# Summing squares along rows, with few idle products, at the head of an attention-and-GELU kernel

## The chip, the cores and the metric

One core of a Trainium2 chip (trn2). The metric is the device time of one execution in microseconds (us). Each version is run several times on the same chip as the version it is compared with; one execution is profiled, and every execution lists the mean clock granted to TensorE.

## The reference

Four batches of q, k, v with 6080 rows and 256 columns; then a two-layer network with a tanh GELU on all 24320 rows of the attention's output.

```python
qn = q / (np.linalg.norm(q, axis=1, keepdims=True) + 1e-06)   # norm of each column over 6080 rows
kn = k / (np.linalg.norm(k, axis=1, keepdims=True) + 1e-06)
s = kn.transpose(0, 2, 1) @ qn / tau                          # 256 x 256 scores
a = softmax(s)                                                # over the last axis
x = (v @ a).reshape(B * S, D)
h = x @ w_in                                                  # 256 -> 2048
out = gelu_tanh(h) @ w_out                                    # 2048 -> 256
```

Scores and weights can be merged (a @ w_in is 256 x 2048), so the long part of the kernel is two products per block of 512 rows. But the first block can start only when batch 0's scores are known, and these need every row of q and k of batch 0: their product G and the column sums of squares. That head is what the change is about.

## The kernel before

Batch 0 is loaded in ten chunks of 2, 12, 12, 5 (and a rest), 4, 4, 4, 2, 1, 1 slots of 128 rows. For each chunk VectorE casts q and k to bf16, ScalarE squares them, and TensorE adds k^T q to G (two products of 256 columns per slot) and the squares to `cols`. A column of sums is made by a product whose weights are the squares and whose moving operand is one column of ones:

```python
def col_sums(cols, x, ones, first, last):
    for m in range(4):                       # q and k, two halves of 128 columns each
        nc.tensor.matmul(cols[:, m : m + 1],
                         lhsT=x[m // 2][:, m % 2 * 128 : m % 2 * 128 + 128], rhs=ones, ...)

fillers = [0, 0, 0, 5, 6, 5, 4, 2, 1, 0]     # idle products, chunk by chunk

def keep_clock(n):                           # bf16, 512 columns, result unused
    ...
for n, ch in enumerate(first_chunks):
    ...                                      # casts on VectorE (GpSimd for k of chunks 6 and 7)
    ...                                      # squares on ScalarE (VectorE for q of 6 and 7)
    keep_clock(fillers[n])
    for s, rows in slots_of(ch, 128):
        gram(G, qkb, s, rows, ...)           # two products of 256 columns
    ...                                      # pairs of squares added on VectorE, then col_sums
```

The twelve-slot chunks have one tile for q and one for k. Then come the norms, the scaled scores, their transposes, exp, the first pieces of `aw` (softmax @ w_in), and the first block's products `hp`. v of block 0 is turned on TensorE into one PSUM tile of two halves of 512 columns, and the first pieces of aw are scaled in halves, VectorE and ScalarE by turns:

```python
vps = pH.tile([128, 2, 512], FP32, tag="h", name="vps")
...
nc.vector.tensor_copy(vT0[:, 0, :], vps[:, 0, :])
...
nc.scalar.activation(vT0[:, 1, :], vps[:, 1, :], AF.Copy)
...
for n, t, act in ((0, 0, False), (1, 0, True), (0, 1, True), (1, 1, False), (2, None, False), (3, None, False)):
    ...                                      # aw piece = ps * 1/row sum, on ACT where act, else on DVE
```

Later batches are prepared while the products of the batch before run, and are the same in both versions.

## Time and profile before

| | before |
|---|---|
| time, median of 3 runs | 753.54 us (753.44 to 753.94) |
| span of the profiled run | 751.6 us |
| TensorE busy | 727.2 us (97%) |
| the loads of q and k of batch 0 end | about 34.7 us |
| sums of squares end | 37.48 us |
| first four hp products issued (start of the products after them) | 42.50 us |

TensorE is "PE" in the profile, VectorE "DVE", ScalarE "ACT", GpSimd "POOL". In a line of the chain of waits the columns are start, length and the work. In a line of a window they are its bounds, its length, the busy time of PE, PEld, DVE, ACT and POOL (with the instructions started), and at the end PEclk (granted clock, 1.00 is full), the DMA share and GB/s. The last row of the table is the *mark* used below: from it on TensorE hardly rests (in the run before it is busy for 692.84 of the 697.50 us from the mark to 740 us), and 751.6 - 42.50 = 709.1 us follow it.

### The profile page before, as it was taken

How to read it: one execution, taken by the hardware profiler on the slowest of the kernel's cores; microseconds unless marked ns; L12 is line 12 of the kernel's file. 1: busy time of each engine (PE TensorE's matmuls, PEld its weight loads, DVE VectorE, ACT ScalarE, POOL GpSimd, SP SyncE). 2: the span in 40 equal slices, each digit the busy share in tenths (PEclk: the TensorE clock that was granted, in tenths of full speed). 3: DMA queues.
4: the chain of work that ended last, by engine and by line, in shares of the span. 5: the costliest groups of instructions: out<-in, count | busy, mean ns of one | idle time of the engine just before them, and what ended most of it. 6: DMA issues, size and time to landing. Idle time of an engine off the chain costs nothing.

```text
span 751.6 us, 12382 instructions
## 1 busy us (share of the span) xinstructions
PE 727.2 (97%) x5181; PEld 502.5 (67%) x5271; DVE 289.9 (39%) x513; ACT 419.6 (56%) x414; POOL 82.3 (11%) x159
## 2 busy tenths in 40 slices
PE   3899999999999999999999999999999999999998
PEld 2656667666666666766666666776666666666666
DVE  4643646463431645554341265555343011011011
ACT  5675555555556555555645555555564655555552
POOL 1161110101012102101001102010101000000000
PEclk9999999999999999999999999999999999999999
DMA  8979676613227685833325776671422533321111
GB/s 373 386 226 175 120 144 144 132 43 79 83 62 144 113 162 108 142 79 81 87 57 116 145 115 125 148 143 46 76 81 56 103 88 67 69 78 50 41 57 57
DMA packets 83111, 86.48 MB, mean 115 GB/s; under 512 B 58992, under 2 KB 61680, under 8 KB 82544
## 3 DMA queue, kind: packets, MB, share of 16 engines
q0 software_dynamic: 14480, 30.87, 25.9%
q1 hardware_dynamic: 68272, 54.49, 24.8%
q8 instruction: 41, 0.67, 0.4%
q10 hardware_dynamic: 304, 0.33, 0.1%
q14 instruction: 14, 0.11, 0.1%
HBM read 78.91 MB, written 24.90 MB: 138 GB/s over the span
## 4 chain that ended last, share of the span: by engine, by line
PE 96%; DMA 2%; issue 1%; DVE 1%; SPq 0%; ACT 0%; DVEq 0%
PE yp L572 44%; PE hp L646 43%; PE G L177 5%; DMA st<-in_k_dram 2%; PE ps L229 2%; PE idle L173 1%; PE cols L189 0%; PE yp L677 0%; DVE qk L277 0%; SPq L83 0%; PE T L399 0%; DVE vT L404 0%; DVE Gs L207 0%; ACT aw L440 0%; PE vps L391 0%
## 5 line engine op out<-in xcount | busy, mean ns | idle before, releaser
L650 ACT ACTIVATE g<-hp 128x1024 bf16<-128x1024 f32 (+1 forms) x384 | 389.4, 1014 | 305.9 <-PE hp L646 292.0
L572 PE MATMUL yp<-wout_bf,g 128*128 128x256 bf16 x3024 | 392.0, 273 | 1.0
L646 PE MATMUL hp<-vT,aw 128*128 128x512 bf16 (+1 forms) x1453 | 383.3, 377 | 3.8 <-ACT aw L440 0.2
L572 PEld LDWEIGHTS <-g 128*128 128x128 bf16 x3024 | 295.9, 98 | 113.4
L646 PEld LDWEIGHTS <-aw 128*128 128x128 bf16 x1536 | 150.0, 98 | 104.2 <-ACT aw L440 0.4
L589 DVE COPY ysb<-yp 128x512 f32<-128x512 f32 (+1 forms) x95 | 64.9, 683 | 393.9 <-PE yp L572 393.9
L489 DVE TENSOR_TENSOR acc<-acc,sq 128x512 f32<-128x512 f32 x141 | 97.6, 692 | 4.8
L488 DVE TENSOR_TENSOR sq<-qkb 128x512 bf16<-128x512 bf16 x141 | 58.9, 418 | 0.0
L177 PE MATMUL G<-qkb 128*128 128x256 bf16 x288 | 55.0, 273 | 0.0
L313 POOL DMA_DIRECT2D vb<-in_v_dram x47 | 25.9, 553 | 90.3 <-DMA vT<-vb 84.3
L338 POOL CAST gate<-g 1x1 f32<-1x1 bf16 x24 | 5.9, 244 | 232.8 <-ACT g L650 232.8
L235 DVE TENSOR_SCALAR aw<-ps,rsinv 128x512 bf16<-128x512 f32 x30 | 22.4, 749 | 22.2 <-PE ps L229 15.8
L177 PEld LDWEIGHTS <-qkb 128*128 128x128 bf16 x288 | 28.2, 98 | 3.3
L177 PE MATMUL G<-qk 128*128 128x256 bf16 x96 | 15.6, 324 | 14.7 <-DVE qk L277 14.7
L177 PEld LDWEIGHTS <-qk 128*128 128x128 bf16 x96 | 10.7, 115 | 18.8 <-DVE qk L277 14.9
L229 PE MATMUL ps<-win_bf,eT 128*128 128x512 bf16 x54 | 16.4, 379 | 0.1
L508 POOL TENSOR_TENSOR r<-r,half 128x4 f32<-128x4 f32 x3 | 3.1, 1040 | 101.6 <-DVE r L507 101.6
L279 ACT ACTIVATE sq<-st 128x3072 bf16<-128x3072 f32 (+2 forms) x6 | 10.6, 1768 | 5.8 <-DMA st<-in_k_dram 2.6
L83 POOL DMA_DIRECT2D qkb<-in_q_dram x24 | 12.8, 535 | 5.8 <-issue 4.3
L83 POOL DMA_DIRECT2D qkb<-in_k_dram x24 | 13.0, 542 | 0.0
L629 POOL COPY g<-gr 128x1024 bf16<-128x1024 bf16 x2 | 2.1, 1034 | 98.2 <-PE yp L572 98.2
L664 POOL COPY gr<-g 128x1024 bf16<-128x1024 bf16 x2 | 2.1, 1035 | 79.9 <-ACT g L650 79.9
(84 smaller groups left out, 137.8 us busy)
## 6 DMA issues: line engine op xcount, KB each, us to landing
out_dram<-ysb SPq DMA_DIRECT2D x44, 512.0 KB, 3.0
vb<-in_v_dram POOLq DMA_DIRECT2D x43, 256.0 KB, 6.6
qkb<-in_q_dram POOLq DMA_DIRECT2D x21, 384.0 KB, 4.6
qkb<-in_k_dram POOLq DMA_DIRECT2D x21, 384.0 KB, 6.4
vT<-vb SPq DMA_TRANSPOSE x184, 2.9
wst<-in_moe_w_out_dram SPq DMA_DIRECT2D x4, 512.0 KB, 10.4
g<-in_q_dram SPq DMA_DIRECT2D x1, 1536.0 KB, 6.8
g<-in_k_dram SPq DMA_DIRECT2D x1, 1536.0 KB, 10.0
```

The costliest lines, as they stand in the source:

```text
L83: engines[x].dma_start(out=dst[x][:, 0:size, :], in_=src[b, s0 * 128 : (s0 + size) * 128, :].rearrange("(p s) c -> p s c", s=size))
L177: nc.tensor.matmul(G[:, ic, :], lhsT=qk[1][:rows, s, ic * 128 : ic * 128 + 128], rhs=qk[0][:rows, s, :], start=first and ic == 0, stop=las ...
L229: nc.tensor.matmul(ps, lhsT=eT[:, jc, ic * 128 : ic * 128 + 128], rhs=win_bf[:, jc, fs * 512 : fs * 512 + 512], start=jc == 0, stop=jc == 1)
L235: nc.vector.tensor_scalar_mul(dst, sorted_columns(ps, fs), rsinv[:, ic : ic + 1])
L279: nc.scalar.activation(sq[:, 0:hi] if whole is None else sq, x, AF.Square)
L313: nc.gpsimd.dma_start(out=t[:, 0:n, :], in_=v_rows[r0 : r0 + n * 128, :].rearrange("(p s) c -> p s c", s=n))
L488: nc.vector.tensor_mul(sq[:rows], flat, flat)
L489: nc.vector.tensor_add(acc[:rows], acc[:rows], sq[:rows])
L572: nc.tensor.matmul(yp[:rows, at, :], lhsT=g[:, fc, s * 128 : s * 128 + rows], rhs=wout_bf[:, fc, :], start=fc == 0, stop=fc == FC - 1)
L589: nc.vector.tensor_copy(ysb[:, s0 : s + 1, :], yp[:, 0 : s + 1 - s0, :])
L646: nc.tensor.matmul(hp[:, j, :cols], lhsT=aw[:, cc, fc * 128 : fc * 128 + 128], rhs=vT[:, cc, :cols], start=cc == 0, stop=cc == 1)
L650: nc.scalar.activation(g[:, 2 * i : 2 * i + 2, :cols], hp[:, :, :cols], AF.Gelu_apprx_tanh)
```

## The change

The intent: the head's TensorE spends 23 idle products on its clock and many tiny products on sums. The change (1) sums the squares of chunks 0 to 4 along rows, one product of 512 columns per pair of slots with a column of ones as weights, copies the row out of PSUM once and turns it into columns by four fp32 products; (2) keeps three idle products, now fp32; (3) gives the twelve-slot chunks two tiles that hold q and k of six slots each; (4) does chunk 6's and 7's casts of k on VectorE, leaves chunk 7's square of q to ScalarE, and lets VectorE add the squares of chunks 4 and 5 in pairs too; (5) gives the halves of v block 0 own PSUM tiles and scales the first aw pieces whole. The change was also described with "later scores turned by DMA", but both versions do that alike. The core of the diff, with cuts:

```diff
-    fillers = [0, 0, 0, 5, 6, 5, 4, 2, 1, 0]
-    SQUARES_DVE = (6, 7)
-    CASTS_POOL = (6, 7)
+    IN_ROWS, SQUARES_DVE = 5, 6
+    fillers = [0, 0, 0, 1, 1, 1, 0, 0, 0, 0]
...
-    filler = const.tile([128, 512], BF16)
+    filler = const.tile([128, 1, 256], FP32)
...
+    row = pY.tile([128, 512], FP32, tag="y", name="row")[0:1, :].rearrange("p (x c) -> p x c", c=256)
+    row_sb = accp.tile([128, 2, 256], FP32, tag="acc", name="row_sb")[0:1]
...
+    def row_sums_of(parts):
+        nonlocal rowed
+        for x in parts:
+            nc.tensor.matmul(row, lhsT=ones_bf, rhs=x, start=rowed == 0, stop=rowed == n_sums - 1)
+            rowed += 1
+        if rowed == n_sums:
+            nc.vector.tensor_copy(row_sb, row)
+
+    def turn_rows():
+        for m in range(4):
+            nc.tensor.matmul(cols[:, m : m + 1], lhsT=row_sb[:, m // 2, m % 2 * 128 : m % 2 * 128 + 128],
+                             rhs=ones_f[0:1, :], start=m == 0, stop=False, skip_group_check=True)
...
+        qks = [qkp.tile([128, 2, SMAX, 256], BF16, tag="qk", name="qk") for _ in range(n_tiles)]
+        sqs = [sqp.tile([128, 2, SMAX, 256], BF16, tag="sq", name="sq") for _ in range(n_tiles)]
...
-    vps = pH.tile([128, 2, 512], FP32, tag="h", name="vps")
+    vps = [pH.tile([128, 2, 512], FP32, tag="h", name="vps")[:, 0, :] for _ in range(2)]
...
-    for n, t, act in ((0, 0, False), (1, 0, True), (0, 1, True), (1, 1, False), (2, None, False), (3, None, False)):
+    for n in range(4):
```

More of the change, by code (lines that the diff above doesn't have):

```diff
@@ L99 @@
     n_chunks = len(first_chunks)
-    TAIL = 4
-    fillers = [0, 0, 0, 5, 6, 5, 4, 2, 1, 0]
-    SQUARES_DVE = (6, 7)
-    CASTS_POOL = (6, 7)
-    def halves(pool, tag, dtype, size, most=SMAX):
-        tiles = [pool.tile([128, 2, most, 256], dtype, tag=tag, name=tag)
-                 for _ in range(1 if size <= most else 2)]
-        if len(tiles) == 1:
-            return [tiles[0][:, x] for x in range(2)], tiles[0]
-        return [t.rearrange("p a b c -> p (a b) c") for t in tiles], None
+    IN_ROWS, SQUARES_DVE = 5, 6
+    fillers = [0, 0, 0, 1, 1, 1, 0, 0, 0, 0]
     def slot_pair(whole, lo, hi):
@@ L167, in pieces @@
         return dst.rearrange("a (e t p) -> a e t p", p=128, t=t_of(fs))
-    def keep_clock(n, pool=pH, tag="h"):
+    def keep_clock(n):
         for _ in range(n):
-            idle = pool.tile([128, 2, 512] if pool is pH else [128, 512], FP32, tag=tag, name="idle")
-            nc.tensor.matmul(idle[:, 0, :] if pool is pH else idle, lhsT=filler[:, 0:128], rhs=filler, start=True, stop=True)
+            idle = pH.tile([128, 2, 512], FP32, tag="h", name="idle")
+            nc.tensor.matmul(idle[:, 0, :], lhsT=filler[:, 0, 0:128],
+                             rhs=filler.broadcast_to([128, 2, 256]), start=True, stop=True)
     def gram(G, qk, s, rows, first, last):
@@ L178, in gram @@
                 G[:, ic, :],
-                lhsT=qk[1][:rows, s, ic * 128 : ic * 128 + 128],
-                rhs=qk[0][:rows, s, :],
+                lhsT=qk[:rows, 1, s, ic * 128 : ic * 128 + 128],
+                rhs=qk[:rows, 0, s, :],
                 start=first and ic == 0,
@@ L239, with col_sums_of, pairs_of @@
     cols = pA.tile([128, 512], FP32, tag="a", name="cols")
-    seen, summed = 0, 0
-    def sums_of(parts, last):
-        nonlocal summed
+    row = pY.tile([128, 512], FP32, tag="y", name="row")[0:1, :].rearrange("p (x c) -> p x c", c=256)
+    row_sb = accp.tile([128, 2, 256], FP32, tag="acc", name="row_sb")[0:1]
+    n_sums = sum(-(-size // 2) + rem for _, size, rem in first_chunks[:IN_ROWS])
+    rowed = 0
+    def row_sums_of(parts):
[9 more added lines that the diff above has]
+                             rhs=ones_f[0:1, :], start=m == 0, stop=False, skip_group_check=True)
+    def col_sums_of(parts, last=False):
         for m, x in enumerate(parts):
-            col_sums(cols, x, ones_bf[: x[0].shape[0], :], summed == 0, last and m == len(parts) - 1)
-            summed += 1
-    def pairs_of(n, sqb):
-        size = first_chunks[n][1]
+            col_sums(cols, [x[:, y] for y in range(2)], ones_bf, False, last and m == len(parts) - 1)
+    def pairs_of(sq, size, rem):
         h = size // 2
-        pair, whole = halves(prp, "pair", BF16, h, SMAX // 2)
-        for x in range(2):
-            nc.vector.tensor_add(pair[x][:, 0:h], sqb[x][:, 0:h], sqb[x][:, h : 2 * h])
-        parts = [[y[:, s, :] for y in pair] for s in range(h)]
-        if size % 2:
-            parts.append([y[:, size - 1, :] for y in sqb])
-        if first_chunks[n][2]:
-            parts.append([y[:, size, :] for y in sqb])
-        sums_of(parts, False)
+        pair = prp.tile([128, 2, SMAX // 2, 256], BF16, tag="pair", name="pair")[:, :, 0:h]
+        nc.vector.tensor_add(pair, sq[:, :, 0:h], sq[:, :, h : 2 * h])
+        return [pair[:, :, s] for s in range(h)] + [sq[:, :, s] for s in range(2 * h, size + rem)]
+    seen = 0
     waiting = None
@@ L264 @@
         st, whole = staged[n]
-        size = ch[1]
-        qkb, qk_whole = halves(qkp, "qk", BF16, size)
-        sqb, sq_whole = halves(sqp, "sq", BF16, size)
-        hi = size + ch[2]
+        _, size, rem = ch
+        n_tiles = -(-size // SMAX)
+        each = size // n_tiles
+        hi = each + rem
+        qks = [qkp.tile([128, 2, SMAX, 256], BF16, tag="qk", name="qk") for _ in range(n_tiles)]
+        sqs = [sqp.tile([128, 2, SMAX, 256], BF16, tag="sq", name="sq") for _ in range(n_tiles)]
@@ L269 @@
         if whole is None:
-            todo = list(zip(qkb, sqb, st))
+            todo = [(x, t, st[x][:, t * each : t * each + each]) for x in range(2) for t in range(n_tiles)]
         else:
-            todo = [[y[:, :, 0:hi] for y in (qk_whole, sq_whole, whole)]]
-        if n in CASTS_POOL:
-            nc.gpsimd.tensor_copy(qkb[1][:, 0:hi], st[1])
-            todo = [(qkb[0][:, 0:hi], None, st[0])]
-        for to, sq, x in todo:
-            nc.vector.tensor_copy(to[:, 0:hi] if whole is None else to, x)
-            if sq is not None and n not in SQUARES_DVE:
-                nc.scalar.activation(sq[:, 0:hi] if whole is None else sq, x, AF.Square)
@@ L280 @@
-        if n in SQUARES_DVE:
-            nc.scalar.activation(sqb[1][:, 0:hi], st[1], AF.Square)
-            nc.vector.tensor_mul(sqb[0][:, 0:hi], qkb[0][:, 0:hi], qkb[0][:, 0:hi])
-        keep_clock(fillers[n])
-        for s, rows in slots_of(ch, 128):
-            gram(G, qkb, s, rows, seen == 0, seen == n_all - 1)
-            seen += 1
+            todo = [(slice(0, 2), 0, whole)]
+        for x, t, src in todo:
+            nc.vector.tensor_copy(qks[t][:, x, 0:hi], src)
+            if n != SQUARES_DVE or x == 1:
+                nc.scalar.activation(sqs[t][:, x, 0:hi], src, AF.Square)
@@ L287, with waiting @@
+        if n == SQUARES_DVE:
+            nc.vector.tensor_mul(sqs[0][:, 0, 0:hi], qks[0][:, 0, 0:hi], qks[0][:, 0, 0:hi])
+        keep_clock(fillers[n])
+        for t in range(n_tiles):
+            for s in range(hi):
+                gram(G, qks[t], s, 128, seen == 0, seen == n_all - 1)
+                seen += 1
+        if n == IN_ROWS + 1:
+            turn_rows()
         if waiting is not None:
-            pairs_of(*waiting)
+            waiting()
             waiting = None
         if n < 3:
-            pairs_of(n, sqb)
-        elif n < TAIL:
-            waiting = (n, sqb)
+            for t in range(n_tiles):
+                row_sums_of(pairs_of(sqs[t], each, rem))
+        elif n <= IN_ROWS:
+            def waiting(n=n, sq=sqs[0], each=each, rem=rem):
+                (row_sums_of if n < IN_ROWS else col_sums_of)(pairs_of(sq, each, rem))
@@ L294 @@
         else:
-            sums_of([[y[:rows, s, :] for y in sqb] for s, rows in slots_of(ch, 128)], n == n_chunks - 1)
+            col_sums_of([sqs[0][:, :, s] for s in range(hi)], n == n_chunks - 1)
     v0 = stage.tile([128, 2, SMAX, 256], FP32, tag="st", name="v0")
@@ L348, in load_qk @@
             load_chunk((nc.gpsimd, nc.gpsimd), views, b, later_chunks[n])
-            loaded_of[b, n] = views, t
+            loaded_of[b, n] = t
     w_homes = []
@@ L385 @@
     Gs = scaled(G, r)
-    vps = pH.tile([128, 2, 512], FP32, tag="h", name="vps")
-    spare = pH.tile([128, 2, 512], FP32, tag="h", name="spare")
+    vps = [pH.tile([128, 2, 512], FP32, tag="h", name="vps")[:, 0, :] for _ in range(2)]
     def turn_v0(cc):
         for s in range(4):
-            nc.tensor.matmul(vps[:, cc, s * 128 : s * 128 + 128],
+            nc.tensor.matmul(vps[cc][:, s * 128 : s * 128 + 128],
                              lhsT=v0[:, s, cc * 128 : cc * 128 + 128],
@@ L403 @@
     vT0 = vts.tile([128, 2, 512], BF16, tag="vT", name="vT")
-    nc.vector.tensor_copy(vT0[:, 0, :], vps[:, 0, :])
+    nc.vector.tensor_copy(vT0[:, 0, :], vps[0])
     eT = smx.tile([128, 2, 256], BF16, tag="eT", name="eT")
@@ L408 @@
         nc.scalar.activation(eT[:, jc, :], T[jc][:, 0:256], AF.Exp, scale=r[:, jc : jc + 1])
-    nc.scalar.activation(vT0[:, 1, :], vps[:, 1, :], AF.Copy)
+    nc.scalar.activation(vT0[:, 1, :], vps[1], AF.Copy)
     firsts = []
@@ L425 @@
     first_aw(1, 0)
-    rsinv = row_sums(eT, spare[:, 0, :])
+    rsinv = row_sums(eT, pH.tile([128, 2, 512], FP32, tag="h", name="rs")[:, 0, :])
     first_aw(0, 1)
@@ L435 @@
         ps = firsts[n][:, 0:256].rearrange("a (p t) -> a t p", t=2)
-        if t is not None:
-            dst, ps = dst[:, t], ps[:, t]
         scale = rsinv[:, ic : ic + 1]
-        if act:
+        if n == 1:
             nc.scalar.activation(dst, ps, AF.Copy, scale=scale)
@@ L478, in attention_steps @@
             load_qk(b, n + 2)
-            qk, whole = loaded_of.pop((b, n))
+            qk = loaded_of.pop((b, n))
             for s, rows in slots_of(ch, 128):
@@ L482, in attention_steps @@
                 gram(G, qk, s, rows, first, last)
-                flat = whole[:rows, :, s, :]
+                flat = qk[:rows, :, s, :]
                 if first:
```

## The prediction

> **What bounds the kernel now.** I read the page first (busy shares, chain), then the chain in order of time for the first 75 us, then windows of 1 us and the timelines of VectorE and ScalarE there. The page:
>
> ```profile
> PE 727.2 (97%) x5181; PEld 502.5 (67%) x5271; DVE 289.9 (39%) x513; ACT 419.6 (56%) x414; POOL 82.3 (11%) x159
> PE 96%; DMA 2%; issue 1%; DVE 1%; SPq 0%; ACT 0%; DVEq 0%
> ```
>
> TensorE is the bound, and 43% + 44% of the span is the products hp and yp, which the diff leaves alone. In the stretch from 700 to 740 us TensorE is busy 39.79 of 40 us. So the change can only move the moment at which the steady products start (about 42 us); after that everything shifts as one block. 2% would be 15 us, more than a third of all that comes before that moment.
>
> The chain of waits from 19 us on (start, length, what):
>
> ```profile
> 19.07 1.77 DVE qk L277
> 20.89 4.22 PE G L177 x24
> 25.11 0.58 PE cols L189 x24
> 25.76 1.03 PE idle L173 x4
> 26.79 1.31 PE G L177 x12
> 28.10 1.30 PE idle L173 x6
> ...
> 37.38 0.09 PE cols L189 x4
> 37.50 0.18 ACT r L382
> ```
>
> Up to 19 us the loads of q and k set the pace (DMA share about 1.0). From 20.89 to 37.48 TensorE never waits, although the last k chunk has landed by 34.68, where its cast starts. So TensorE is in arrears there by its own work, and part of it are idle products: on the chain 1.03 + 1.30 + 1.10 + 0.89 + 0.45 + 0.24 = 5.01 us. The other cause is its clock (columns: length, busy times, then PEclk):
>
> ```profile
> 20.00:21.00 1.00, 0.12 (x1) 0.12 (x2) 1.00 (x2) 1.00 (x1) 0.00 (x0) 0.71 1.02 420
> 21.00:22.00 1.00, 1.00 (x6) 0.69 (x6) 0.77 (x2) 0.89 (x1) 0.00 (x0) 0.50 1.00 378
> 23.00:24.00 1.00, 1.00 (x7) 0.74 (x6) 1.00 (x1) 1.00 (x1) 0.00 (x0) 0.58 1.04 414
> 24.00:25.00 1.00, 1.00 (x14) 0.90 (x12) 0.60 (x1) 1.00 (x1) 0.00 (x0) 1.00 1.01 401
> ```
>
> 0.71 means that the clock fell at 20.42, 0.58 that it came back at 23.83. [...] TensorE had stood still from 18.56 to 20.89. The 24 products of chunk 2 took 4.22 us; at the full-clock pace of chunk 3 (12 in 1.31) they take 2.62, so 1.6 us are lost.
>
> After the sums, the start of the steady products hangs on these (VectorE, then ScalarE waits, then the products):
>
> ```profile
> 40.17 0.69 DVE L404 CAST vT<-vps 128x512 bf16<-128x512 f32 x1 [0.97 <-PE vps L391]
> 40.89 0.60 ACT L409 ACTIVATE vT<-vps 128x512 bf16<-128x512 f32 x1 [0.43 <-DVE vT L404]
> 41.78 1.14 DVE L442 TENSOR_SCALAR aw<-ps,rsinv 128x128 bf16<-128x128 f32 x3 [0.37 <-ACT aw L440]
> 42.06 0.61 PE L646 MATMUL hp<-vT,aw 128*128 128x512 bf16 x2 [0.20 <-ACT aw L440]
> ```
>
> [...] 23.83 - 20.42 = 3.41 us at 0.50. [...] while GpSimd casts chunk 7, VectorE's cast of 128x512 takes 0.73 us (0.41 for chunk 8) and its square 0.82 (a 128x512 product elsewhere 0.42).[...]
>
> **The change, part by part.** The words about later scores turned by DMA describe something that both versions have; the diff does not touch it.
>
> 1. *Idle products.* 23 bf16 ones fall to 3 fp32 ones of 512 columns. A 512-column pass is 0.215 us (four hp in 0.86)[...].
>
> 2. *Row sums.* For chunks 0 to 4 each pair of slots now is one product of 512 columns with a column of ones as weights, 0.215 us, in place of four products of one column, 4 x 0.024 = 0.10 (24 in 0.58). Counts: 1 + 6 + 6 + 4 + 2 = 19, of which 12 (chunks 2, 3, 4) come after 20 us: 12 x 0.215 = 2.58. Before, column products there took 0.58 + 0.78 + 0.38 x 2 + 0.18 + 0.08 + 0.09 = 2.47; the 40 that remain (8 + 16 + 8 + 4 + 4) take 0.96. Four small products turn the row, about 0.2. Sum: 2.58 + 0.96 + 0.2 - 2.47 = +1.3 us. [...]
>
> 3. *Chunks 1 and 2 in two tiles of both q and k.* A cast of 3072 columns takes 1.76, of 2048 1.23, of 1024 0.69: slope 0.52 ns a column, so 1536 take 0.96. The products of a first half can start at 19.07 + 0.96 + 0.02 = 20.05, not 20.89: -0.84. For chunk 1 likewise 12.65, not 13.49. With the same clock phase its grams end near 17.4 and six row products near 18.7. In the window 17.0 to 20.4 TensorE then streams about 2 of 3.4 us instead of about 1[...], which may keep the clock up. I give that 0.65.
>
> 4. *VectorE and GpSimd.* GpSimd's casts of chunks 6 and 7 go to VectorE. Its list from the end of the row sums: copy of the row (0.69, as the 512-column PSUM reads), chunk 6 casts 0.69 + 0.69, square 0.69, pairs of chunk 5 0.69, cast of chunk 7 0.69, chunks 8 and 9 0.41 each: 4.96, less about 0.08 overlap at each of seven joints, 4.4 us. Before, from chunk 6 on, 3.8. The row copy stands ahead of chunk 6's casts in VectorE's order, so these now wait for TensorE's last row product.
>
> 5. *Halves of v in own tiles.* VectorE's copy can run right after Gs (39.2) and ScalarE's right after eT (40.46), not at 40.89. The row-sum reciprocal (40.78) still waits for TensorE. Then aw is scaled in whole 128x256 pieces: VectorE from 41.06 for 0.48, ScalarE beside it for an estimated 0.47 (0.366 for 128 columns plus 128 x 0.83 ns, the slope of the squares). The four first hp products run 41.56 to 42.42 without a gap, where before they ended at 42.67. Gain 0.25. ScalarE's table load starts about 0.4 earlier too, but TensorE is the bound there.
>
> **Sum, if the clock stays up.** Grams of chunk 2 20.05 to 22.6; its rows wait for the second pair (22.95), end 23.9; filler, chunk 3 to 26.05; filler, chunk 4 to 27.8; rows of chunk 3 28.6; filler, chunk 5 30.35; last rows 30.8. VectorE: 30.85 + 4.4 = 35.3, barely after the last landing (34.65). TensorE then has chunks 7, 8, 9, 8 products of 0.109 and 16 small ones, 1.25 us from 34.7: sums end at 36.0 instead of 37.48, -1.45. With part 5: -1.7.
>
> **If the clock falls as before.** Chunk 2 takes about 1.7 us longer, the last row product ends at 32.7, VectorE 32.75 + 4.4 = 37.15, sums end near 37.7: +0.2, and with part 5 about 0.
>
> **The rivals.** (A) *The arrears move to VectorE:* the row copy holds up the casts, as in the cold case. For it: 4.4 us of VectorE work after the last row product; against: slack of about 1 us when the clock is up. Result 753.5. (B) *The clock falls later:* chunks 6 to 9 have no fillers, and in the warm case TensorE idles from 30.8 to 32.8. One window at half clock around 34 to 37 or at the start of the steady products costs up to 3.41/2 = 1.7 us and eats the gain: 753.3 to 753.6. Against: before, 38 to 42 us was only 2.92 of 4 us busy, partly with transposes, and the clock stayed at 1.00. (C) *Transfers bound the head anyway:* the last landing stays at 34.65, so nothing beyond 37.48 - 34.65 less cast, two products and sums (about 0.8), 2.0 us, can be won. Together with part 5 that is 751.3, the floor. (D) *A gain at 42 us is given back*, because weights or v land late. wout's last cast ends at 51.0 and is first used after 53.7, so 1.7 us earlier still fits.
>
> **Range and chances.** 0.65 x -1.7 + 0.35 x 0 = -1.1; rival B takes back about 0.1. So 753.54 - 1.0 = 752.5 us. The low end, 751.6, is the warm case in full with some 0.2 more; the high end, 753.7, the cold case plus noise (the three runs of before span 0.5). Neither 738 nor 769 is in reach: 0.99 for within 2%.
>
> **What would show it.** Right: PEclk at 1.00 from 21 to 24; first gram product of chunk 2 near 20.0; sums ended near 36;[...] the first four hp without a gap and the rest an unchanged block. Wrong: PEclk 0.50 in chunk 2 again or at 34 to 44; chunk 6's casts on VectorE behind the row copy later than 32 us; or a different time after 50 us at equal starts, which nothing here accounts for.

The forecast's sum came to -1.7 us at full clock and, weighed, to -1.0 us, 752.5 us: part 1 had put the idle products at 2.4 us less on the chain, and with the +1.3 of part 2 TensorE's work from chunk 2 on came to 13.8 us in place of 14.9. The sum's times still leave about 0.85 us for each of the three fp32 idle products (23.9 to 26.05, less 1.31 for chunk 3). That was my assumption, which no run had shown by then. The chance of 0.65 for a clock that stays up was my estimate, too.

## The result, and the profile after

| | before | after |
|---|---|---|
| time, median of 4 runs | 753.74 us (753.44 to 754.56) | 756.92 us (755.63 to 757.07) |
| span of the profiled run | 751.6 | 755.1 |
| mean granted clock, profiled run | 0.997 | 0.993 |
| grams of chunk 2 start | 20.89 | 20.19 |
| sums of squares end | 37.48 | 38.75 |
| mark | 42.50 | 45.79 |
| span less mark | 709.1 | 709.3 |

The ratio is 1.0037 (95% interval 1.0019 to 1.0054): slower by 0.4%, which counts as the same at 2%, where a gain of 1.0 us was predicted. A ratio here is the mean time of one kernel's runs over that of the other's in the same rounds, so not quite the ratio of the medians. The last row says that next to nothing happened after the mark: of the 3.5 us between the spans, 3.3 us lie before it, in the head.

The chain of waits of the changed kernel, in order of time:

```profile
19.18 0.97 DVE qk L277
20.19 2.79 PE G L168 x24
22.99 1.39 PE row L241 x6
...
31.36 0.54 PE row L241 x2
...
31.92 0.68 DVE row_sb L244
32.59 1.21 DVE qk L277 x2
...
33.85 1.05 PE G L168 x8
34.90 0.98 PE cols L248 x8
...
38.65 0.10 PE cols L180 x4
...
44.29 1.71 PE hp L648 x4
```

Chunk 2 goes as hoped: grams from 20.19, 2.79 us in place of 4.22. But where TensorE's arrears ran through to the end of the sums, the chain now leaves it at 31.9: VectorE copies the row, and only then casts chunk 6. TensorE stands still until 33.85. And the first four hp take 1.71 us where four took 0.86. The windows of 1 us of the changed kernel say why:

```profile
32.00:33.00 1.00, 0.00 (x0) 0.00 (x0) 1.00 (x2) 0.00 (x0) 0.00 (x0) 1.00 1.08 378
35.00:36.00 1.00, 1.00 (x15) 0.98 (x16) 1.00 (x4) 0.63 (x1) 0.00 (x0) 0.97 1.07 371
36.00:37.00 1.00, 1.00 (x26) 0.87 (x23) 0.27 (x1) 0.32 (x1) 0.50 (x1) 0.50 1.04 371
40.00:41.00 1.00, 0.49 (x3) 0.39 (x4) 1.00 (x3) 0.45 (x2) 1.00 (x2) 0.50 1.03 389
46.00:47.00 1.00, 1.00 (x5) 0.39 (x4) 0.37 (x1) 0.96 (x1) 0.31 (x1) 0.91 1.07 211
```

By the same reading as in the prediction (0.97: half clock for the last 0.06; 0.91: for the first 0.18) the clock fell at 35.94 and came back at 46.18, after 10.2 us, three times 3.41.

**Theory 1:** the pause and the missing idle products let the clock fall, and the clock is nearly all of the loss. **Theory 2:** the held-up casts are the loss, by delay; the clock only goes with them. **Others:** the two-tile casts, the work moved to VectorE, or the last part cost time.

### The profile page after: what moved, and what is told of

It reads as the page before. It is cut to its first block, busy times and chain, and to the rows that moved or that the text cites. A ratio compares the mean times of both kernels' runs of the same rounds, so it can differ in the third digit from the quotient of the medians.

```text
span 755.1 us, 12306 instructions
## 1 busy us (share of the span) xinstructions
PE 735.4 (97%) x5189; PEld 502.0 (66%) x5189; DVE 291.5 (39%) x517; ACT 420.5 (56%) x417; POOL 80.5 (11%) x157
## 4 chain that ended last, share of the span: by engine, by line
PE 96%; DMA 2%; DVE 1%; SPq 0%; issue 0%; ACT 0%; DVEq 0%
PE yp L574 44%; PE hp L648 44%; PE G L168 5%; DMA st<-in_k_dram 2%; PE ps L220 2%; PE idle L163 0%; PE row L241 0%; DVE qk L277 0%; PE cols L180 0%; PE yp L679 0%; PE ps L422 0%; SPq L83 0%; PE T L403 0%; PE cols L248 0%; PE vps L395 0%; DVE r L191 0%
## 5 line engine op out<-in xcount | busy, mean ns | idle before, releaser
L648 PE MATMUL hp<-vT,aw 128*128 128x512 bf16 (+1 forms) x1536 | 391.6, 377 | 0.0
L279 ACT ACTIVATE sq<-st 128x1536 bf16<-128x1536 f32 (+3 forms) x9 | 11.9, 1337 | 7.8 <-DMA st<-in_k_dram 4.9
L548 DVE RECIPROCAL den<-den 128x256 f32<-128x256 f32 x6 | 10.5, 1753 | 0.2
```

The source lines that it names most:

```text
L279: nc.scalar.activation(sqs[t][:, x, 0:hi], src, AF.Square)
L648: nc.tensor.matmul(hp[:, j, :cols], lhsT=aw[:, cc, fc * 128 : fc * 128 + 128], rhs=vT[:, cc, :cols], start=cc == 0, stop=cc == 1)
```

## The experiments

All twelve runs gave correct results. Runs 1 to 8 were on one chip, 9 to 11 on a second, 12 on a third; each chip has its own runs of the kernel before. The differences are a few tenths of a per cent, so intervals and spreads matter.

### 1. Two more idle products, in the pause

```diff
-    fillers = [0, 0, 0, 1, 1, 1, 0, 0, 0, 0]
+    fillers = [0, 0, 0, 1, 1, 1, 2, 0, 0, 0]
```

> The changed kernel with two more idle fp32 products ahead of chunk 6's gram products, in the stretch in which TensorE stood idle (31.9 to 33.85 us). Nothing else differs. Theory 1 (the clock is the cause: that idle stretch lets the granted clock fall for three windows of 3.41 us, from 35.97 to 46.18): PEclk stays at 1.00 from 30 to 47 us, the sums end near 37.0 to 37.4 instead of 38.74, and the time is 753.0 to 753.8, that is 3 to 3.5 us below the changed kernel. Theory 2 (the row copy ahead of chunk 6's casts on VectorE is the cause by itself, the clock only follows): the casts are as late as before, and the time stays at 756 to 757. If the clock still falls, but later or for fewer windows, 755 to 756.

Measured: 753.68 us (753.62 to 753.72, 4 runs), ratio to before 1.0001 (0.9983 to 1.0019). The chain of waits and two windows of this kernel:

```profile
31.95 0.68 DVE row_sb L244
32.63 1.21 DVE qk L277 x2
...
33.89 1.05 PE G L168 x8
```

```profile
36.00:37.00 1.00, 1.00 (x33) 0.95 (x31) 0.31 (x1) 0.32 (x1) 0.54 (x1) 1.00 1.05 375
40.00:41.00 1.00, 0.98 (x12) 0.58 (x11) 0.08 (x1) 1.00 (x3) 1.00 (x2) 1.00 1.06 397
```

Row copy and casts are as late as in the changed kernel, and chunk 6's grams start at the same moment (33.89 against 33.85). Only the clock differs: 1.00 throughout. The mark is at 42.76, not 45.79, so the clock was worth 3.0 of the 3.3 us (0.5 of it in a step of VectorE that took 0.68 us beside a cast on GpSimd, and 0.17 here, see run 4). Theory 1 holds; theory 2, which left the time at 756 to 757, falls as the explanation of the loss. The sums end at 37.89, later than I expected (37.0 to 37.4), and with the clock held the change is only as fast as the kernel before.

### 2. The row copied by ScalarE

```diff
-            nc.vector.tensor_copy(row_sb, row)
+            nc.scalar.activation(row_sb, row, AF.Copy)
```

> The changed kernel with the copy of the row out of PSUM on ScalarE in place of VectorE, so that chunk 6's casts need not wait for TensorE's last row product. Theory 2 (the held-up casts set the end of the sums and make the idle stretch): chunk 6's casts run at 29.8 to 31, its gram products follow the last row product at about 31.9 without the idle 1.96 us, and the sums end at 35.5 to 36.5 with the clock up; time 751.3 to 752.5. Theory 1 says the same of the idle stretch, but warns: there are no idle products after chunk 5[...], so the clock may fall somewhere from 34 to 46 us in some runs; a run with one window at half clock would be up to 1.7 us longer, with three 753.5 to 755.

Measured: 752.35 us (751.63 to 753.77), ratio 0.9986 (0.9967 to 1.0005). The timeline of this kernel (start, length, engine, line, what), and two windows:

```profile
31.94 1.05 PE L168 MATMUL G<-qk 128*128 128x256 bf16 x8
32.04 0.59 ACT L244 ACTIVATE row_sb<-row 1x512 f32<-1x512 f32 x1 [2.07 <-PE row L241]
```

```profile
35.00:36.00 1.00, 1.00 (x22) 0.92 (x21) 0.00 (x0) 0.60 (x3) 0.00 (x0) 0.95 1.05 369
36.00:37.00 1.00, 0.91 (x4) 0.51 (x3) 0.69 (x3) 0.98 (x2) 0.49 (x1) 0.50 1.04 383
```

The pause is gone: chunk 6's grams start at 31.94, and the sums end at 35.94. So the place of one 0.68 us copy in VectorE's order made the 1.96 us pause. Yet the clock fell in the profiled run all the same, for one window (35.90 to about 39.3), although TensorE's records show it busy all through the window before. So a pause is not needed. What fills that window is mostly products of one column. By my count (8 grams in 0.87 us, so 0.109 each), of the 3.41 us before the fall only some 1.2 us stream: the last three of chunk 6's grams and the eight of chunks 7 to 9. A product of one column is counted as nothing: by its columns it is 1/256 of a gram, an estimated 0.0004 us, while on the chain it takes 0.024 us (24 in 0.58, in the run before). That is an estimate of 35%. It is one execution: the other three have a mean clock of 0.999 or 1.000, and one lost window (1.7 of 752 us) would lower it by 0.002.

The mark is at 41.33, 4.5 us before the changed kernel's, but the span only 3.2 us shorter: 710.6 us follow the mark, 1.5 more than in run 1. The list of waits of TensorE (us in total, times, longest) names where it went:

```profile
PE hp L648 <- DMA vT<-vb: 1.3, 1, 1.3
```

Block 2's v, turned by DMA, came too late for so early a start. I had ruled out such a give-back in the prediction (rival D) after looking at the weights alone.

### 3. The kernel before without its late idle products

```diff
-    fillers = [0, 0, 0, 5, 6, 5, 4, 2, 1, 0]
+    fillers = [0, 0, 0, 5, 6, 5, 0, 0, 0, 0]
```

> The kernel before with its seven idle products of chunks 6, 7 and 8 taken out (4, 2 and 1), nothing else. TensorE was in arrears there, so by work alone the sums end up to 7 x 0.22 = 1.5 us earlier: 752.0 to 752.5 if the clock stays up. If those idle products are what holds the clock up (theory 1 in its strong form), it falls at 34 to 46 us and the time is 754 to 757.

Measured: 751.95 us (751.31 to 752.63), ratio 0.9979 (0.9962 to 0.9995), the only ratio below 1 whose interval leaves 1 out. The mark is at 40.52, and the clock stayed up throughout the head in the profiled run. So dropping the late idle products is right by itself where nothing holds the casts up: TensorE pauses just 0.7 us before chunk 6. The strong form of theory 1, that those seven products hold the clock up, falls: two of the four runs have a mean clock of 1.000 without them (the other two 0.997; where these lost a window is not known).

The clock stayed up at chunk 2, too:

```profile
20.00:21.00 1.00, 0.00 (x0) 0.00 (x0) 1.00 (x2) 1.00 (x1) 0.00 (x0) 1.00 1.02 415
21.00:22.00 1.00, 0.91 (x9) 0.82 (x10) 0.90 (x2) 1.00 (x1) 0.00 (x0) 1.00 1.03 394
```

Yet up to chunk 5 this is the kernel before. But the first rise in its clock record is at 19.64 us (17.01 in the run before); chunk 1's grams took 5.30 us (4.49), and the pause ahead of chunk 2 was only 1.49 us (2.32). So the fall at chunk 2 comes in some executions only; of the 26 executions of the kernel before beside these experiments, 10 have a mean clock of 0.999 or more and so lost no window, if one lost window lowers it by 0.002. Part of the 2.0 us between the two marks is this luck: run 9, with the same edit, the last part and the clock fallen at chunk 2, has its mark at 40.95.

### 4. The last part alone, on the kernel before

The edit is the last two hunks of the diff above.

> The kernel before with the change's last part alone: the halves of v block 0 in own PSUM tiles, and the first pieces of aw scaled as whole 128x256 pieces. By my sum: the four first hp products without a gap, 0.25 us gained, time 753.1 to 753.6. A rival: ScalarE's or VectorE's longer pieces delay the first hp product by more than the missing gaps return: 753.7 to 754.2.

Measured: 753.55 us (753.42 to 754.98), ratio 1.0004 (0.9987 to 1.0021): nothing to be seen in the time. In the trace the four hp run without a gap, as predicted, but the first of them starts later. From the end of the sums (here the end of the last column product in the timeline) to the mark the runs without the part need 42.50 - 37.46 = 5.04 us (before) and 40.52 - 35.61 = 4.91 (run 3), those with it 4.88 (this run: 42.59 - 37.71; run 8 below: 40.50 - 35.62). So it gains 0.03 us. The other 0.13 between before and run 3 is VectorE's first step of the norms, on 128x4 numbers: it takes 0.17 us in run 3, with nothing on GpSimd beside it, but 0.30 in the run before, from 37.70 to 38.00, where GpSimd's casts of w_in end at 37.98. In the changed kernel the same two lines of the timeline read:

```profile
38.59 1.04 POOL L375 CAST win_bf<-wst 128x1024 bf16<-128x1024 f32 x1 [0.70 <-DMA wst<-in_moe_w_in_dram]
38.97 0.68 DVE L191 TENSOR_SCALAR r<-r 128x4 f32<-128x4 f32 x1 [2.70 <-ACT r L387]
```

It ended at 39.65, just after GpSimd at 39.63, 0.5 us longer than 0.17. Run 12 has the same (0.73, end 39.62, GpSimd 39.59); where the sums ended at another moment and no cast ran beside it, as in runs 1, 5 and 6, it took 0.17. I read this as a collision of the two; why the step is longer the traces do not show.

### 5. No idle products at all

```diff
-    fillers = [0, 0, 0, 1, 1, 1, 0, 0, 0, 0]
+    fillers = [0, 0, 0, 0, 0, 0, 0, 0, 0, 0]
```

> The changed kernel with no idle product at all (its three fp32 ones of chunks 3, 4 and 5 out as well). TensorE's last row product then ends some 1.5 to 2 us earlier (about 30, when chunk 4's pairs are added), so the row copy no longer holds up chunk 6's casts much. If the cause is the held-up casts, the sums end near 36.5 at full clock and the time is 751.5 to 752.5. If the clock is the cause[...], the clock falls again before 46 us, for one to three windows, as there is nothing to fill TensorE's pauses: 753.5 to 757.

Measured: 755.12 us (754.23 to 755.81), ratio 1.0024 (1.0003 to 1.0044). The granted clock is 0.993 to 0.997; it fell in the profiled run at 34.1 for two windows. The timeline:

```profile
32.77 1.05 PE L168 MATMUL G<-qk 128*128 128x256 bf16 x8 [1.98 <-DVE qk L277]
```

I had expected that an earlier last row product would free the casts. It ended 1.1 us earlier, and chunk 6's grams came 1.1 us earlier too, after the same pause of 1.98 us. The pause is built in: here as in the changed kernel (copy from 31.92, casts from 32.59, gram at 33.85) copy and two casts run one after the other between the last row product and the next gram.

### 6. One idle product in the pause

```diff
-    fillers = [0, 0, 0, 1, 1, 1, 0, 0, 0, 0]
+    fillers = [0, 0, 0, 1, 1, 1, 1, 0, 0, 0]
```

> The changed kernel with one idle fp32 product ahead of chunk 6's gram products (two held the clock up in every run). It fills about half of the 1.96 us pause. If half is enough, the time is like that with two, 753.4 to 753.8, with little spread. If the window's threshold lies between, some runs hold and some fall, and the runs spread from 753.5 to 757. If one is not enough, 756 to 757.

Measured: 753.85 us (753.72 to 754.00), ratio 1.0004 (0.9989 to 1.0019), clock 1.000 in all four runs. TensorE still pauses for 0.92 us. One was enough, in these four runs.

### 7. Columns in place of rows, the rest of the change kept

```diff
-            nc.tensor.matmul(row, lhsT=ones_bf, rhs=x, start=rowed == 0, stop=rowed == n_sums - 1)
+            col_sums(cols, [x[:, y] for y in range(2)], ones_bf, rowed == 0, False)
...
-        if n == IN_ROWS + 1:
-            turn_rows()
```

> The changed kernel with its row sums undone alone: the first sums go into columns again (four products of one column per pair), with no row copy and no turning; tiles, idle products and the last part as changed. Chunk 6's casts then wait for nothing but their data (about 31). My view of the row products: they stream and keep the clock up between chunks 1 and 2, and by column products it falls at about 20 us for one window (PEclk 0.50 at 21 to 24) in most runs; at the end there is less to hold the casts up, so TensorE pauses less. Time 751.5 to 753. If the loss of the change lies in something else than the row copy and the missing idle products (the two-tile casts, GpSimd's casts moved to VectorE), the clock falls as in the changed kernel and the time stays at 755 to 757.

Measured: 752.70 us (752.12 to 753.05), ratio 0.9988 (0.9972 to 1.0003). Undoing the row sums alone takes 4.2 us off the changed kernel. So the two-tile casts, the casts moved to VectorE and the three fp32 idle products do no harm that shows. Three windows show what the rows were good for:

```profile
20.00:21.00 1.00, 0.73 (x7) 0.66 (x8) 1.00 (x3) 1.00 (x2) 0.00 (x0) 0.99 1.02 415
21.00:22.00 1.00, 1.00 (x7) 0.67 (x6) 0.95 (x2) 1.00 (x1) 0.00 (x0) 0.50 1.04 397
36.00:37.00 1.00, 0.63 (x5) 0.40 (x5) 0.86 (x4) 1.00 (x1) 0.38 (x1) 1.00 0.92 302
```

Here, with column products, the clock fell at chunk 2 (20.98 to 24.40), as in the profiled runs of the kernel before and of runs 4 and 9; in runs 3 and 11, with columns too, it did not. In all seven profiled runs with rows it stayed up. One of them, run 5, has its window where the kernel before has it (reckoned from its fall at 34.11, 17.05 to 20.46; before, 17.01 to 20.42). So that half of the idea worked. But next to nothing came of it, as TensorE's arrears from chunk 2 are worked off by the time the last chunks land: here the sums end at 35.71 in spite of it.

### 8. A bridge over the early pause

The kernel before with eight idle products ahead of chunk 2, none after chunk 5, and the last part.

```diff
-    fillers = [0, 0, 0, 5, 6, 5, 4, 2, 1, 0]
+    fillers = [0, 0, 8, 5, 6, 5, 0, 0, 0, 0]
```

> A candidate for the better version: the kernel before without its idle products after chunk 5 (alone 751.95), with eight bf16 idle products in TensorE's pause between chunks 1 and 2, and with the change's last part (own tiles for v's halves, whole aw pieces). If TensorE's pause at 18.5 to 20.9 us is what lowers the clock in chunk 2, PEclk stays 1.00 there in every run, and with the 0.15 us that the last part took off, the time is 751.0 to 752.0. If data bounds the sums (last landing 34.7) the bridge gains nothing, and only the spread gets smaller: 751.5 to 752.2.

Measured: 751.97 us median, runs 751.79, 759.28, 752.16, 751.46; ratio 1.0001 (0.9954 to 1.0049), useless because of the one run. The clock of that run was 0.995; nothing here explains its 7 us. The profiled run has the clock at 1.00 throughout the head and its mark at 40.50, as run 3 (40.52). Since run 3 kept the clock without the bridge, this pair does not show what the bridge does. Run 9, the same kernel without it on another chip, says more: all six of its executions have a clock of 0.995 to 0.998, while here three of four have 0.999. Its clock fell at chunk 2, and its sums end at 36.07 in place of 35.62. So the bridge holds the clock there (1.00 from 21 to 22 us in run 8, 0.50 in run 9), and that is worth some 0.45 us between these two traces.

### 9 to 11. Candidates for a better version

Run 9 is run 3 with the last part. Run 11 is run 9 with v block 2 loaded together with block 1. Run 10 is run 2 (row copy on ScalarE) with one idle product ahead of chunk 6, so the change with both repairs. The edit of run 9, to the kernel before, beside the last part:

```diff
-    fillers = [0, 0, 0, 5, 6, 5, 4, 2, 1, 0]
+    fillers = [0, 0, 0, 5, 6, 5, 0, 0, 0, 0]
```

> The kernel before with its idle products after chunk 5 taken out (alone 751.95) and with the change's last part (alone 0.15 us earlier by the trace, nothing in the time): a candidate for the better version, without the bridge. If the two add up, 751.3 to 752.2, ratio to before 0.997 to 0.999. If the time is set by block 2's transposed v (it waited 0.2 us there without the last part), the last part gives nothing: the same 751.9 as without it.

Measured: 752.85 us (752.12 to 754.13, 6 runs), ratio 0.9992 (0.9974 to 1.0010). The two do not add up to anything beyond run 3, and run 3's gain does not show again: the interval holds 1. The edit of run 10, to the changed kernel:

```diff
-            nc.vector.tensor_copy(row_sb, row)
+            nc.scalar.activation(row_sb, row, AF.Copy)
...
-    fillers = [0, 0, 0, 1, 1, 1, 0, 0, 0, 0]
+    fillers = [0, 0, 0, 1, 1, 1, 1, 0, 0, 0]
```

> The changed kernel with both repairs: the row copy on ScalarE, and one idle fp32 product ahead of chunk 6's gram products. With the row copy on ScalarE alone the clock still fell in the profiled run (at 35.95), though TensorE stood still nowhere: in the window before, most of its instructions were products of one column. If streaming work per window is what counts, the idle product of 0.86 to 1.05 us holds the clock up in all runs: spread below 1 us, time 752.3 to 753.2 (one idle product later than the best runs of the ScalarE copy alone, 751.6). If pauses counted and not streaming, the idle product gives nothing and the spread stays at 2 us.

Measured: 752.72 us (752.53 to 752.88), ratio 0.9987 (0.9968 to 1.0006). The spread shrank from 2.1 us to 0.35, and the clock was 0.999 or 1.000 in all four runs. This fits theory 1 in the form "streaming work per window", against the form "no pauses". But of run 2's four executions only one had lost a window, and the spreads are those of two chips, so it is weak support; the count after run 12 says more. The edit of run 11, to that of run 9:

```diff
-        if fs % 2:
-            load_v(1 + fs // 2)
+        if fs == 1:
+            load_v(1)
+            load_v(2)
```

> As the candidate of this call (few idle products and the last part), with the load of v block 2 issued with that of block 1, ahead of the last two casts of w_in on GpSimd, some 3 us earlier. If the last 0.2 to 0.3 us lie in block 2's transposed v, its wait vanishes and the time falls by as much, 751.0 to 751.9. If the earlier load only takes bandwidth from w_out, which GpSimd casts and TensorE needs from 51 us on, the time stays or rises by some tenths.

Measured: 752.91 us (752.09 to 753.43, 6 runs), ratio 0.9989 (0.9973 to 1.0005). The wait for block 2's v did not vanish; it was 1.0 us in the profiled run, and TensorE waited another 0.3 for a cast of w_in. My reason for that last wait was wrong or incomplete, and what makes the turned v late stays open.

### 12. The changed kernel again

No edit.

> The changed kernel itself once more, with its own runs of the kernel before, as the first runs may have been on another chip than the experiments. If the fall of the clock after 34 us belongs to the kernel and not to one chip or to luck with the window's phase, nearly all runs are at 755.5 to 757 with a mean granted clock of 0.993 to 0.995, against 753 to 754.5 for before. If it was luck, some runs are near 753.7 with a clock of 0.999, as the kernel with two more idle products has them.

Measured: 756.90 us (755.05 to 757.12), ratio 1.0035 (1.0018 to 1.0051), on a third chip. The profiled run happened to be the shortest of the four. Two windows of it:

```profile
36.00:37.00 1.00, 1.00 (x25) 0.81 (x22) 0.22 (x1) 0.40 (x1) 0.55 (x1) 0.71 1.03 374
39.00:40.00 1.00, 0.60 (x3) 0.20 (x1) 0.86 (x3) 1.00 (x1) 1.00 (x2) 0.59 1.02 375
```

Fallen at 36.42, back at 39.82: one window. This gives a scale: no window at half clock 753.7 (run 1), one 755.05 (clock 0.998), three 756.9 to 757.1 (clock 0.993). In all eight executions of the changed kernel, the first four and these, the mean clock was 0.993 to 0.998 and the time at least 755.05, so none was like run 1.

*What streams in each window, counted in all traces.* The clock record of each trace gives the window's edges in every profiled run (in the run before the rise at 23.84 and the last fall at 750.88 are 727.04 us apart, 213 times 3.413). For the 114 windows at full clock up to about 50 us in the fourteen traces, the streaming was estimated as in run 2: 0.109 us for a product of 256 bf16 columns or an fp32 transpose of 128 (four in 0.45 on the chain of the run before), others in proportion, nothing for products of one column. In the eight windows after which the clock fell, this is 22 to 37% of the window (37% in run 2, with the start of a transpose counted in); in the 106 after which it stayed up, 38% or more. The busy time does not separate them: 42 to 100% before a fall, from 57% on where the clock stayed up. In the changed kernel the window before the fall has 26%; the lowest in run 6, with one idle product more, has 38%, in run 1, with two, 41%. The transposes have to be counted: without them the window from 37.5 to 40.9 of the run before (ten transposes) and that from 34.63 to 38.05 of run 7 (twelve, and four grams) would each have an estimated 15%, less than any window after which the clock fell, and it stayed at 1.00 after both. So in this head, by this estimate, the clock goes with the streaming per window, and not with pauses. Where exactly a limit lies, an estimate of this kind cannot say.

The marks put together, from the profiled runs (us):

| version | mark | span | span less mark |
|---|---|---|---|
| before | 42.50 | 751.6 | 709.1 |
| changed | 45.79 | 755.1 | 709.3 |
| 12, changed again | 44.09 | 753.2 | 709.1 |
| 1, two idle products more | 42.76 | 751.9 | 709.1 |
| 10, both repairs | 41.86 | 751.0 | 709.1 |
| 2, row copy on ScalarE | 41.33 | 751.9 | 710.6 |
| 7, columns | 40.58 | 750.3 | 709.7 |
| 3, few idle products on before | 40.52 | 749.9 | 709.4 |

Down to a mark of 41.9 the rest is always 709.1 to 709.3. Earlier marks are paid back in part. No version beat the kernel before by more than about 0.2%. Run 3 is the best supported of them, and it is a removal of seven idle products. Runs 9 and 11 contain that removal, and their intervals hold 1, so even this gain is not settled.

## Why the prediction was wrong, point by point

- *The part of rival B.* This is the step that failed. I saw that chunks 6 to 9 had no fillers and that TensorE would pause, but gave it 0.1 us in the sum and "one window", 1.7 us at most. It was three windows in most runs, and 3.0 us by run 1. I had argued from a stretch that was 2.92 of 4 us busy and stayed at full clock. But TensorE's busy time is no measure here: in run 2 it was busy for 4.00 of the 4 us from 31 to 35 and the clock fell at 35.90, as one-column products fill the record (0.024 us each) and stream next to nothing (an estimated 0.0004). The window that I argued from (37.5 to 40.9) streamed an estimated 49%, fp32 transposes included.
- *Three windows, not one.* Once down, the clock stayed down while the sums ended and the scores were turned, and came back after a window in which TensorE was busy for all of each us from 43 to 46. Why one window in some runs and three in others is open: I count 73% of streaming for the first window at half clock here, after which the clock stayed down, and 72% for that of run 12, after which it came back.
- *The fall at chunk 2, taken for a fixed part.* I took TensorE's pause from 18.56 to 20.89 for the cause of the fall. Runs 3 and 11 stood still there as well, for 1.5 us, and kept the clock. A window ends there at 19.64 and 19.43, about where the pause begins; in the four profiled runs in which the clock fell one ends at 20.43 to 20.98, with 1.75 us or more of pause. So by these six traces it goes with where the windows lie. (A slip beside it: the cast of 0.73 us that I quote for GpSimd's work on chunk 7 ran beside its cast of chunk 6, at 31.83 to 32.87.)
- *Rival A, wrongly tied to the cold case.* I wrote that the row copy holds up the casts only if chunk 2 ran at half clock. Run 5 shows that the pause is there no matter when the last row product ends; with the clock up in chunk 2 it was 1.96 us, as my own times (30.8 to 32.8) said. I read the pause as slack, not as the cause of the next thing.
- *Terms of the sum for a full clock.* Run 1 is that case: its sums end at 37.89, not 36.0, and the predicted gain is gone without any fall of the clock (ratio 1.0001). Run 2, with the row copy moved, ends them at 35.94, so the held-up casts are most of this. Turning the row took 0.98 us in eight instructions, not 0.2. The last row product ended at 31.9, not 30.8: grams of chunk 2 at 22.99 rather than 22.6, idle fp32 products of 0.86 to 1.05 instead of about 0.85, row products of 0.23 instead of 0.215.
- *The last part.* 0.25 us were predicted, 0.03 measured. I compared an issue end (42.42) with a modelled completion (42.67); with one kind of end on both sides the gain nearly disappears.
- *What was right.* TensorE bounds the kernel and only the head can matter; chunk 2's grams from 20.05 (20.19) at full clock, and the row products as the reason (runs 5 and 7); the steady products an unchanged block; the time within 2%. Rival C's floor held: no mark came before 40.5. Rival D, dismissed, is real for early marks (runs 2 and 11), by v and not by the weights.

## What to carry to other kernels

Before removing idle products, list what TensorE streams in each 3.41 us up to the start of steady work, and count one-column products as nothing: here the clock fell after windows with an estimated 22 to 37% and stayed up after those with 38% or more. A small copy put into an engine's queue can hold up what stands behind it: here the row copy on VectorE started only at 31.92, after the last row product, and chunk 6's casts behind it at 32.59. Put it on the engine that has nothing due, here ScalarE (chunk 6's grams at 31.94 in place of 33.85). When a change makes one stage earlier, check every later transfer for slack, not just the obvious ones (in run 2 block 2's v cost 1.3 us).
